# Attention scores computed once per batch, block transposes on VectorE and state rows through DRAM, in an attention and top-1 routing kernel

## Chip, cores and metric

The kernel runs on one core of a Trainium2 chip. The metric is the device time of one execution in microseconds (us); lower is better. Engines are named as in the profile: PE is TensorE (matrix products), PEld its weight loads, DVE is VectorE, ACT is ScalarE, POOL is GpSimd, SP is SyncE. PSUM is the memory that PE writes to, in eight banks of 512 float32 columns per partition; SBUF is the working memory.

## What is computed

Two blocks follow one another. The attention block has 8 batches, 8 heads, 512 tokens, 32 states and 64 dimensions per head; every token reads from the states and every state reads from the tokens:

```
scores = 0.125 * x @ state^T;   a  = softmax over the 32 states;   xread = a  @ state
scores2 = 0.125 * state @ x^T;  a2 = softmax over the 512 tokens;  sread = a2 @ x
attn_out = concatenate([xread, sread], axis=2)         # 544 rows per batch and head
```

The result, seen as 4352 rows of 512 values, goes through a switch layer with 8 experts: the row's logits are `x @ w_gate`, the expert with the largest logit is taken, and the row of the output is `gate * (relu(x @ w1[e]) @ w2[e])`, w1 being 512 by 1024 and w2 1024 by 512. Everything is float32. Note that `scores2` is `scores` transposed.

## The kernel before

The work has two stages on the same engines.

**Attention and routing** (lines 128 to 342) goes batch by batch, in a loop at lines 334 to 342. The order in which an engine gets its instructions is fixed before the run, by the framework's scheduler: it takes the instruction that is ready by its own estimate of durations, and of several the one that stands first in the program. So work of neighbouring batches is interleaved, and an engine then runs its list strictly in that order. For batch b+1 the loop calls `weights` (line 325), and then finishes batch b:

- `transpose_x` (162): 16 PE transposes (line 167) turn the tokens into columns, four to a PSUM tile, each tile copied to SBUF by `evict` (120), which takes ACT (line 124) and DVE (line 126) in turn.
- `prep_state` (149): transposes of the states (152) and state times w_gate (158).
- `read_weights` (171): 16 products with the tokens as weights and 64 state columns (line 178), in two halves of 512 score columns per partition. Then, on DVE, the maximum (181), the subtraction (183), the sum (186), a small add (187) and the reciprocal (188); on ACT the exponential (184); on POOL the scaling (189). A token lies on a partition, the states along it.
- `write_weights` (202): the same scores once more, transposed, with the states as weights (64 columns) and 512 token columns (line 209); maximum (212), exponential with the sum (215), reciprocal (217) and scaling (218).
- `transpose_read` (192) and `transpose_write` (221): 8 PE transposes each (198, 227), two PSUM tiles each, evicted into `aT` and `a2T`.
- `read_rows` (282): four tiles `px` of 512 columns (288), evicted into `row`; the logits (294) from `aT` and the product of line 158; then `route`.
- `write_rows` (302): 32 products of 32 state columns by 64 values of x (line 308), all into the 32 partitions that belong to the batch. After batches 3 and 7, 128 state rows are transposed (315), multiplied by w_gate (320) and routed.
- `route` (231): some fifteen short DVE instructions, three sets of counting products (257 to 262) and one indirect DMA on POOL's queue per 128 rows (274), which scatters the rows to their expert's place in a DRAM table. The counts in `base_e` tie each call to the one before.

A float32 product appears in the trace as two PE instructions with a weight load each, a PE transpose as one. PSUM has one set of pools for the whole kernel: `ps_m` four banks, `ps_o` two (px, pw), `ps_s` two (lines 54 to 56). SBUF tiles have two buffers, x three.

**Experts** (line 392 on): when all rows are routed, DVE works out a table of 24 tiles of 256 rows (345 to 388); then for each tile POOL gathers the rows (398), SP loads that expert's weights (407, 409), and PE does transposes (420), the up product (435) and the down product (448); rows leave by indirect DMA (452).

## Time and profile before

| | |
|---|---|
| runs | 932.76, 928.96, 931.94 us; median 931.94 |
| span of the profiled execution, first to last instruction | 925.5 us |
| PE busy | 868.1 us (94%) |
| PEld busy | 609.1 us (66%) |
| DVE busy | 219.8 us (24%) |
| POOL busy | 156.4 us (17%) |
| ACT busy | 99.4 us (11%) |

The profiled execution's own device time is not listed beside its span; the median of the three runs lies 6.4 us above the span, and that difference is taken as what lies around the span. Busy time is the time in which at least one instruction of the engine runs; instructions overlap on PE and slightly on DVE, so that a mean duration is longer than the distance between two starts. "Idle before" names what ended an engine's wait.

### The profile page before, as it was taken

The numbers are of one execution on the slowest core, as the hardware profiler recorded it, in microseconds if no ns is written. First come the engines' busy times: TensorE is split into PE (matmuls) and PEld (weight loads), VectorE is DVE, ScalarE is ACT, GpSimd is POOL, SyncE is SP. The second block draws the span as 40 slices with busy tenths as digits, with TensorE's granted clock in tenths as the row PEclk, the third lists the DMA queues.
The fourth block names the chain that finished last, engine by engine and source line by source line (L and its number), as shares of the span: only waits on it lengthen the run. The fifth ranks groups of instructions, "written<-read, shape, count | busy, mean of one in ns | idle before, by whom it ended". The sixth has DMA issues, their size and how long they took to land.

```text
span 925.5 us, 9941 instructions
## 1 busy us (share of the span) xinstructions
PE 868.1 (94%) x4028; PEld 609.1 (66%) x4028; DVE 219.8 (24%) x628; ACT 99.4 (11%) x196; POOL 156.4 (17%) x166
## 2 busy tenths in 40 slices
PE   2999999990999999999999999999999999999997
PEld 2777877780766677666677666776667766667764
DVE  4456666543111111111111111111111111111110
ACT  1223322220100000000000000000000000000000
POOL 3022332224201111011110111111111101100000
PEclk9899999995799999999999999999999999999999
DMA  9034343117754464554544535545446435355300
GB/s 159 1 84 101 93 103 92 47 47 266 268 204 165 168 215 143 198 186 148 208 171 164 215 128 204 202 136 196 153 160 216 153 146 184 112 196 178 110 0 1
DMA packets 84061, 137.06 MB, mean 148 GB/s; under 512 B 40622, under 2 KB 40622, under 8 KB 84016
## 3 DMA queue, kind: packets, MB, share of 16 engines
q1 hardware_dynamic: 70912, 109.06, 36.5%
q0 software_dynamic: 10400, 26.83, 7.7%
q10 hardware_dynamic: 2704, 0.54, 0.4%
q8 instruction: 32, 0.52, 0.2%
q14 instruction: 13, 0.11, 0.0%
HBM read 122.22 MB, written 21.53 MB: 155 GB/s over the span
## 4 chain that ended last, share of the span: by engine, by line
issue 64%; POOL 9%; PE 3%; DMA 1%; POOLq 1%; DVE 0%
POOL out_dram L452 5%; POOL xg L398 3%; PE ph L435 2%; DMA xg<-xs_dram,grow 1%; PE py L448 1%; POOL xs_dram L274 0%; POOLq L398 0%; POOLq L452 0%; POOLq L496 0%; PE ptx L420 0%; DVE y L451 0%
## 5 line engine op out<-in xcount | busy, mean ns | idle before, releaser
L435 PE MATMUL ph<-fxT,w1t 128*128 128x256 f32 x1536 | 337.4, 381 | 0.0
L448 PE MATMUL py<-w2t,hT 128*128 128x512 f32 x768 | 333.6, 592 | 0.0
L435 PEld LDWEIGHTS ph<-fxT,w1t 128*128 128x128 f32 x1536 | 293.2, 191 | 50.1 <-issue 11.0
L448 PEld LDWEIGHTS py<-w2t,hT 128*128 128x128 f32 x768 | 144.2, 190 | 172.3 <-issue 172.2
L452 POOL DMA_INDIRECT out_dram<-y,ti x48 | 48.6, 1012 | 355.5 <-DVE y L451 323.9
L451 DVE TENSOR_SCALAR y<-py,gw 128x512 f32<-128x512 f32 x48 | 36.0, 751 | 293.6 <-PE py L448 293.6
L398 POOL DMA_INDIRECT xg<-xs_dram,grow x48 | 49.5, 1030 | 252.6 <-PE ptx L420 236.8
L440 ACT ACTIVATE hT<-ph 128x512 f32<-128x512 f32 x48 | 28.7, 597 | 553.0 <-PE ph L435 553.0
L438 DVE TENSOR_SCALAR hT<-ph 128x512 f32<-128x512 f32 x48 | 33.1, 690 | 145.9 <-PE ph L435 145.9
L420 PE MATMUL ptx<-ident,xg 128*128 128x128 f32 x192 | 27.7, 288 | 22.8 <-DMA xg<-xs_dram,grow 22.8
L274 POOL DMA_INDIRECT xs_dram<-row,r_sli x32 | 31.7, 992 | 81.7 <-DVE r_sli L271 30.2
L423 DVE TENSOR_TENSOR ti<-xg,inv_i 128x1 int32<-128x1 int32 x48 | 6.0, 158 | 164.8 <-DMA out_dram<-y,ti 143.0
L420 PEld LDWEIGHTS ptx<-ident,xg 128*128 128x128 f32 x192 | 23.6, 148 | 26.6 <-issue 22.8
L178 PE MATMUL pc<-stT,xT 128*128 128x64 f32 x256 | 37.2, 307 | 0.4 <-ACT stT L124 0.4
L178 PEld LDWEIGHTS pc<-stT,xT 128*128 128x128 f32 x256 | 34.9, 219 | 2.3 <-issue 1.4
L288 PE MATMUL px<-bd,aT 128*128 128x256 f32 x128 | 31.9, 387 | 0.1
L308 PE MATMUL pw<-x_nat,a2T 128*32 128x64 f32 x512 | 30.5, 219 | 0.0
L308 PEld LDWEIGHTS pw<-x_nat,a2T 128*32 128x32 f32 x512 | 28.8, 110 | 1.5 <-ACT r_ex L247 1.3
L189 POOL TENSOR_TENSOR a<-sh,sm 128x512 f32<-128x512 f32 x16 | 16.9, 1059 | 74.9 <-DVE sm L188 73.9
L167 PE MATMUL pt<-ident,x_nat 128*128 128x128 f32 x128 | 20.7, 300 | 7.4 <-DMA x_nat<-in_x_dram 6.8
L288 PEld LDWEIGHTS px<-bd,aT 128*128 128x128 f32 x128 | 22.7, 191 | 3.3 <-DVE aT L126 0.6
L124 ACT COPY fxT<-ptx 128x512 f32<-128x512 f32 x24 | 14.0, 585 | 98.3 <-PE ptx L420 98.3
(121 smaller groups left out, 391.0 us busy)
## 6 DMA issues: line engine op xcount, KB each, us to landing
w1t<-in_moe_w_dram SPq DMA_DIRECT2D x24, 2048.0 KB, 8.9
w2t<-in_moe_w_dram SPq DMA_DIRECT2D x24, 2048.0 KB, 9.1
x_nat<-in_x_dram SPq DMA_DIRECT2D x32, 256.0 KB, 5.1
xg<-xs_dram,grow POOLq DMA_INDIRECT x48, 6.9
out_dram<-y,ti POOLq DMA_INDIRECT x48, 3.1
bd<-in_state_dram ACTq DMA_DIRECT2D x8, 64.0 KB, 4.5
xs_dram<-row,r_sli POOLq DMA_INDIRECT x32, 5.2
xs_dram<-srow,r_sli POOLq DMA_INDIRECT x2, 6.1
```

What stands on the lines that cost most here:

```text
L178: nc.tensor.matmul(pc[:, i, ts(j, 2), :], lhsT=xT[:, j, 2 * u + i, :], rhs=stT[:, b, j, :], start=True, stop=True, skip_group_check=True)
L274: d = nc.gpsimd.indirect_dma_start(out=xs_dram[:], out_offset=bass.IndirectOffsetOnAxis(ap=sli[:, u:u + 1], axis=0), in_=row[:, u, :].bitc ...
L288: nc.tensor.matmul(px[:, ts(g, 256)], lhsT=aT[:, g, c, :], rhs=bd[:, b, g], start=True, stop=True, skip_group_check=True)
L308: nc.tensor.matmul(px[r, ts(h, D)], lhsT=a2T[:, h // 4, c, ts(h % 4, NS)], rhs=x_nat[b][:, c, h, :], start=(c == 0), stop=(c == NC - 1), s ...
L398: nc.gpsimd.indirect_dma_start(out=xg_bufs[(NH * j + k) % XB][:].bitcast(I32), out_offset=None, in_=xs_dram[:], in_offset=bass.IndirectOff ...
L420: nc.tensor.transpose(pt[:, c, :], xg[:, ts(c, 128)], ident[:])
L435: nc.tensor.matmul(ph[:, i, :], lhsT=w1t[:, c, ts(2 * f2 + i, 128)], rhs=xT[:, c, :], start=(c == 0), stop=(c == NDC - 1), skip_group_chec ...
L438: nc.vector.tensor_scalar(hT[:, ts(f2, 2), :], ph[:], 0.0, None, ALU.max)
L440: nc.scalar.activation(hT[:, ts(f2, 2), :], ph[:], AF.Relu)
L448: nc.tensor.matmul(py[:], lhsT=hT[:, f, ts(k, 128)], rhs=w2t[:, f, :], start=(f == 0), stop=(f == NFC - 1))
L451: nc.vector.tensor_scalar(y[:], py[:], gw[:, k:k + 1], None, ALU.mult)
L452: d = nc.gpsimd.indirect_dma_start(out=out[:], out_offset=bass.IndirectOffsetOnAxis(ap=ti[:, k:k + 1], axis=0), in_=y[:], in_offset=None, ...
```

## The change

The scores are computed once per batch, with the states as weights (as line 209 did), into one tile of two PSUM banks. For the softmax over the states, DVE turns every 32x32 block of that tile, so that the 32 states of a head lie along the partition; it does the softmax there over 1024 columns and turns the blocks back, which gives `aT` directly. The 16 products of line 178, the 8 transposes of line 198 and the evictions of `aT` are gone. The softmax over the tokens reads the same PSUM tile; its scaling moves from the weights to the product `pw`. The write product works on pairs of heads: 16 products of 64 state columns by 128 values of x, whose two halves alternate between partitions 0 to 63 and 64 to 127; only the blocks of equal heads are kept. They are scaled from PSUM into `xs` and sent to a DRAM tile by four DMAs on ACT's queue per batch; 128 state rows are read back and routed after batch 5 (batches 0 to 3) and after the last. `write_rows` now stands before `read_rows`. PSUM pools are made anew for each stage: in the attention stage `ps_c` has two tiles of two banks, `ps_m` two banks, `ps_o` and `ps_s` one each; the expert stage has the old sizes. Comments were removed too.

```diff
+    st_dram = dram.tile([B * NS, DM], FP32)
...
-    ps_m = ctx.enter_context(tc.tile_pool(name="ps_m", bufs=4, space=bass.MemoryType.PSUM))
-    ps_o = ctx.enter_context(tc.tile_pool(name="ps_o", bufs=2, space=bass.MemoryType.PSUM))
-    ps_s = ctx.enter_context(tc.tile_pool(name="ps_s", bufs=2, space=bass.MemoryType.PSUM))
+    ps_c = tc.alloc_tile_pool(name="ps_c", bufs=2, space=PSUM)
+    ps_m = tc.alloc_tile_pool(name="ps_m", bufs=2, space=PSUM)
+    ps_o = tc.alloc_tile_pool(name="ps_o", bufs=1, space=PSUM)
+    ps_s = tc.alloc_tile_pool(name="ps_s", bufs=1, space=PSUM)
...
-    def read_weights(b, xT):
...
-    def transpose_read(a):
...
-    def write_weights(b, xT):
...
+    def scores(b, xT):
+        pc = ps_c.tile([128, 2, S], FP32, tag="c", name="pc")
+        for j in range(NPR):
+            nc.tensor.matmul(pc[ts(j % 2, 64), j // 2, :], lhsT=stT[:, b, j, :], rhs=xT[:, j],
+                             start=True, stop=True, skip_group_check=True)
+        return pc
+
+    def read_weights(pc):
+        NB = 2 * S // 32
+        sx = att.tile([128, NB, NS], FP32, tag="sx", name="sx")
+        nc.vector.transpose(sx[:].rearrange("p b n -> p (b n)"), pc[:].rearrange("p g s -> p (g s)"))
+        mx = att.tile([128, NB, 1], FP32, tag="mx", name="mx")
+        nc.vector.tensor_reduce(mx[:, :, 0], sx[:], AX.X, ALU.max)
+        nc.vector.tensor_tensor(sx[:], sx[:], mx[:].to_broadcast([128, NB, NS]), ALU.subtract)
+        nc.scalar.activation(sx[:], sx[:], AF.Exp, bias=0.0, scale=SCALE)
+        sm = att.tile([128, NB, 1], FP32, tag="sm", name="sm")
+        nc.vector.tensor_reduce(sm[:, :, 0], sx[:], AX.X, ALU.add)
+        nc.vector.tensor_scalar(sm[:], sm[:], 1e-9, None, ALU.add)
+        nc.vector.reciprocal(sm[:], sm[:])
+        nc.gpsimd.tensor_tensor(sx[:], sx[:], sm[:].to_broadcast([128, NB, NS]), ALU.mult)
+        aT = att.tile([128, 2, NC, 128], FP32, tag="aT", name="aT")
+        nc.vector.transpose(aT[:].rearrange("p g c q -> p (g c q)"), sx[:].rearrange("p b n -> p (b n)"))
+        return aT
+
+    def write_weights(pc):
+        nm = att.tile([128, 2], FP32, tag="nm", name="nm")
+        nc.vector.tensor_reduce(nm[:], pc[:], AX.X, ALU.max)
+        nc.vector.tensor_scalar(nm[:], nm[:], -SCALE, None, ALU.mult)
+        a2 = att.tile([128, 2, S], FP32, tag="a2", name="a2")
+        s2 = att.tile([128, 2], FP32, tag="s2", name="s2")
         for g in range(2):
+            nc.scalar.activation(a2[:, g], pc[:, g], AF.Exp, bias=nm[:, g:g + 1], scale=SCALE,
+                                 accum_out=s2[:, g:g + 1])
+        nc.vector.tensor_scalar(s2[:], s2[:], 1e-9, None, ALU.add)
+        nc.vector.reciprocal(s2[:], s2[:])
+        return a2, s2
...
-    def write_rows(b, a2T):
...
+    def write_rows(b, a2T, s2):
+        pw = ps_o.tile([128, 2, 2, D], FP32, tag="o", name="pw")
+        for g in range(2):
             for c in range(NC):
+                for i in range(2):
+                    nc.tensor.matmul(pw[ts(i, 64), g], lhsT=a2T[:, g, c, ts(i, 64)],
+                                     rhs=x_nat[b][:, c, ts(2 * g + i, 2), :],
+                                     start=(c == 0), stop=(c == NC - 1), skip_group_check=True)
+        xs = att.tile([128, 2, 2, D], FP32, tag="xs", name="xs")
+        for g in range(2):
+            nc.vector.tensor_scalar(xs[:, g], pw[:, g], s2[:, g:g + 1], None, ALU.mult)
+        for i in range(4):
+            nc.scalar.dma_start(out=st_dram[ts(b, NS)].rearrange("n (g i d) -> n g i d", g=2, i=4)[:, :, i, :],
+                                in_=xs[ts(i, NS), :, i % 2, :])
+
+    def route_states(g4):
+        srow = att.tile([128, 1, XW], FP32, tag="srow", bufs=1, name="srow")
+        nc.scalar.dma_start(out=srow[:, 0, 0:DM], in_=st_dram[ts(g4, 128)])
...
     def weights(b):
         xT = transpose_x(b)
         prep_state(b)
-        return read_weights(b, xT), write_weights(b, xT)
+        pc = scores(b, xT)
+        return read_weights(pc), write_weights(pc)
...
-        a, a2 = soft
+        aT, (a2, s2) = soft
...
-        aT = transpose_read(a)
         a2T = transpose_write(a2)
+        write_rows(b, a2T, s2)
         read_rows(b, aT)
-        write_rows(b, a2T)
+        if b == 5:
+            route_states(0)
+    route_states(1)
...
-    att.release()
+    for pool in (ps_s, ps_o, ps_m, ps_c, att):
+        pool.release()
...
+    ps_m = tc.alloc_tile_pool(name="ps_m2", bufs=4, space=PSUM)
+    ps_o = tc.alloc_tile_pool(name="ps_o2", bufs=2, space=PSUM)
+    ps_s = tc.alloc_tile_pool(name="ps_s2", bufs=2, space=PSUM)
```

What `route_states` does after its DMA is what lines 314 to 323 did.

## Rows read from the trace of the kernel before

**Rows 1.** The page's span in 40 slices, busy tenths of each: PE, DVE.

```profile
PE   2999999990999999999999999999999999999997
DVE  4456666543111111111111111111111111111110
```

**Rows 2.** By stretch: us, busy PE, PEld, DVE, ACT, POOL, granted clock, DMA share, GB/s.

```profile
56.70:77.92 21.22, 20.16 (x190) 17.18 (x189) 13.28 (x43) 6.87 (x15) 6.20 (x6) 1.00 0.46 101
...
168.08:191.20 23.12, 21.40 (x190) 17.41 (x189) 13.86 (x42) 6.68 (x16) 6.06 (x6) 1.00 0.12 46
...
206.05:238.30 32.25, 7.17 (x42) 5.35 (x42) 10.65 (x62) 2.19 (x5) 14.78 (x15) 0.58 0.77 278
238.30:925.50 687.20, 682.19 (x2479) 456.79 (x2477) 92.34 (x205) 41.53 (x70) 88.19 (x87) 1.00 0.46 162
```

**Rows 3.** PE in order of time, one batch (start, us, what, idle before).

```profile
168.08 3.76 PE L308 MATMUL pw<-x_nat,a2T 128*32 128x64 f32 x64
171.77 1.86 PE L167 MATMUL pt<-ident,x_nat 128*128 128x128 f32 x15
...
175.16 0.66 PE L178 MATMUL pc<-stT,xT 128*128 128x64 f32 x4
...
176.75 3.34 PE L178 MATMUL pc<-stT,xT 128*128 128x64 f32 x28
...
181.88 0.66 PE L198 MATMUL pt<-ident,a 128*128 128x128 f32 x4
183.16 0.63 PE L198 MATMUL pt<-ident,a 128*128 128x128 f32 x4 [0.62 <-DVE nm L213]
...
185.86 1.99 PE L288 MATMUL px<-bd,aT 128*128 128x256 f32 x8
187.69 1.40 PE L294 MATMUL pl<-gst,aT 128*128 128x8 f32 x12
```

**Rows 4.** PE in order of time: eight instructions of line 209; a hand-over of a bank.

```profile
109.60 1.94 PE L209 MATMUL pc<-xT,stT 128*64 128x512 f32 x8
...
112.80 0.66 PE L198 MATMUL pt<-ident,a 128*128 128x128 f32 x4 [0.68 <-ACT aT L124]
```

**Rows 5.** Groups by line and shape, 98.98 to 181.5 us (busy us, mean ns).

```profile
L126 DVE COPY row<-px 128x512 f32<-128x512 f32 x7 | 4.8, 691 | 6.0 <-PE px L288 6.0
...
L218 DVE TENSOR_SCALAR a<-a,s 128x512 f32<-128x512 f32 x6 | 2.6, 433 | 0.0
L187 DVE TENSOR_SCALAR sm<-sm 128x16 f32<-128x16 f32 x6 | 2.4, 406 | 0.0
...
L126 DVE COPY stT<-pt 128x128 f32<-128x128 f32 x4 | 1.1, 286 | 0.2
...
L184 ACT ACTIVATE sh<-sh 128x512 f32<-128x512 f32 x7 | 4.4, 630 | 18.1 <-DVE sh L183 18.1
```

**Rows 6.** POOL and DVE around 114 us, in order of time.

```profile
113.67 1.04 POOL L189 TENSOR_TENSOR a<-sh,sm 128x512 f32<-128x512 f32 x1 [2.94 <-DVE sm L188]
...
114.10 0.64 DVE L187 TENSOR_SCALAR sm<-sm 128x16 f32<-128x16 f32 x1
```

**Rows 7.** Line 136, DMA issues on ACT's queue: duration ns min/median/max; landing.

```profile
L136 ACTq DMA_DIRECT2D bd<-in_state_dram x8: 318/330/472, 10.4 to 16.7; - x8
...
DMA to landing us min/median/max: 4.2/4.5/5.5
```

**Rows 8.** The first batch in order of time.

```profile
22.59 1.12 PE L178 MATMUL pc<-stT,xT 128*128 128x64 f32 x4
...
30.33 3.68 PE L209 MATMUL pc<-xT,stT 128*64 128x512 f32 x8
...
50.37 1.03 PE L288 MATMUL px<-bd,aT 128*128 128x256 f32 x4
```

**Rows 9.** Two stretches of 2 us in the first batch (granted clock third from last).

```profile
36.00:38.00 2.00, 1.41 (x11) 0.87 (x9) 2.00 (x7) 1.30 (x4) 1.01 (x2) 1.00 0.03 8
...
42.00:44.00 2.00, 2.00 (x11) 2.00 (x11) 1.35 (x2) 0.50 (x1) 0.00 (x0) 0.50 0.00 0
```

More of the change, by code (lines that the diff above doesn't have):

```diff
@@ L53 @@
     wpool = ctx.enter_context(tc.tile_pool(name="wpool", bufs=2))
[L54 to L56 removed]
+    PSUM = bass.MemoryType.PSUM
     xs_dram = dram.tile([E * NTOK, XW], I32)
+    st_dram = dram.tile([B * NS, DM], FP32)
     ident = const.tile([128, 128], FP32)
@@ L192, in transpose_read @@
-    def transpose_read(a):
-        aT = att.tile([128, 2, NC, 128], FP32, tag="aT", name="aT")
-        for g in range(2):
-            pt = ps_m.tile([128, NC, 128], FP32, tag="m", name="pt")
-            for c in range(NC):
-                nc.tensor.transpose(pt[:, c, :], a[:, c, ts(g, 4), :], ident[:])
-            evict(aT[:, g], pt[:])
-        return aT
-    def write_weights(b, xT):
-        a2 = att.tile([128, 2, S], FP32, tag="a2", name="a2")
-        for g in range(2):
-            pc = ps_m.tile([128, S], FP32, tag="m", name="pc2")
-            for i in range(2):
-                j = 2 * g + i
-                nc.tensor.matmul(pc[ts(i, 64), :], lhsT=stT[:, b, j, :], rhs=xT[:, j],
-                                 start=True, stop=True, skip_group_check=True)
-            nm = att.tile([128, 1], FP32, tag="nm", name="nm")
-            nc.vector.tensor_reduce(nm[:], pc[:], AX.X, ALU.max)
-            nc.vector.tensor_scalar(nm[:], nm[:], -SCALE, None, ALU.mult)
-            s2 = att.tile([128, 1], FP32, tag="s2", name="s2")
-            nc.scalar.activation(a2[:, g], pc[:], AF.Exp, bias=nm[:, 0:1], scale=SCALE, accum_out=s2[:])
-            nc.vector.tensor_scalar(s2[:], s2[:], 1e-9, None, ALU.add)
-            nc.vector.reciprocal(s2[:], s2[:])
-            nc.vector.tensor_scalar(a2[:, g], a2[:, g], s2[:, 0:1], None, ALU.mult)
-        return a2
@@ L296, in read_rows @@
         route(pl[:], row, tok_x[:, b, :], NC)
-    srow = {}
-    def write_rows(b, a2T):
-        g4, r = b // 4, ds(NS * (b % 4), NS)
-        if b % 4 == 0:
-            srow[g4] = att.tile([128, 1, XW], FP32, tag="srow", name="srow")
-        px = ps_o.tile([128, DM], FP32, tag="o", name="pw")
-        for h in range(H):
-            for c in range(NC):
-                nc.tensor.matmul(px[r, ts(h, D)], lhsT=a2T[:, h // 4, c, ts(h % 4, NS)],
-                                 rhs=x_nat[b][:, c, h, :], start=(c == 0), stop=(c == NC - 1),
-                                 skip_group_check=True)
-        evict(srow[g4][r, 0, 0:DM], px[r, :])
-        if b % 4 == 3:
-            pt = ps_m.tile([128, NDC, 128], FP32, tag="m", name="pt")
-            for c in range(NDC):
-                nc.tensor.transpose(pt[:, c, :], srow[g4][:, 0, ts(c, 128)], ident[:])
-            sT = att.tile([128, NDC, 128], FP32, tag="sT", bufs=1, name="sT")
-            evict(sT[:], pt[:])
-            pl = ps_s.tile([128, 1, E], FP32, tag="s", name="pls")
-            for c in range(NDC):
-                nc.tensor.matmul(pl[:, 0, :], lhsT=sT[:, c, :], rhs=wg[:, c, :],
-                                 start=(c == 0), stop=(c == NDC - 1), skip_group_check=True)
-            route(pl[:], srow[g4], tok_s[:, g4:g4 + 1], 1)
@@ new lines, in route_states @@
+    def route_states(g4):
+        srow = att.tile([128, 1, XW], FP32, tag="srow", bufs=1, name="srow")
+        nc.scalar.dma_start(out=srow[:, 0, 0:DM], in_=st_dram[ts(g4, 128)])
+        pt = ps_m.tile([128, NDC, 128], FP32, tag="m", name="pt")
+        for c in range(NDC):
+            nc.tensor.transpose(pt[:, c, :], srow[:, 0, ts(c, 128)], ident[:])
+        sT = att.tile([128, NDC, 128], FP32, tag="sT", bufs=1, name="sT")
+        evict(sT[:], pt[:])
+        pl = ps_s.tile([128, 1, E], FP32, tag="s", name="pls")
+        for c in range(NDC):
+            nc.tensor.matmul(pl[:, 0, :], lhsT=sT[:, c, :], rhs=wg[:, c, :],
+                             start=(c == 0), stop=(c == NDC - 1), skip_group_check=True)
+        route(pl[:], srow, tok_s[:, g4:g4 + 1], 1)
@@ L468 @@
             fetch(j + 2)
-    ffn.release()
+    for pool in (ps_s, ps_o, ps_m, ffn):
+        pool.release()
 _INS = ['x', 'state', 'moe_w_gate', 'moe_w1', 'moe_w2']
```

18 lines of the change are left out of this document (removed).

## Prediction

> **What bounds the kernel now.** I read the 40 slices first [rows 1]: PE is at nine tenths from the second slice to the last but for one hole near 215 to 230 us, and DVE is at five or six tenths in the first eight slices only. So there are two stages. I then cut the span into stretches [rows 2]. The experts take 687.2 us with PE busy in 682.2 of them; the diff gives this stage the PSUM banks that it had, so I leave it alone. The attention stage is six intervals from the write product of batch 0 (56.70) to that of batch 6 (191.20), 134.5 us or 22.4 us each, with PE busy in some 93% and DVE in about 60%. [Rows 2] show the first and the last of the six. A PE-bound stage is the right place to remove PE work. Between 206.05 and 238.30 PE waits for the last scatters, the tile table and the first gathered rows; that tail goes on.
>
> **The change, part by part, per interval, on PE's queue.**
>
> *Read scores removed.* Line 178 is 32 PE instructions per batch, 0.66 + 3.34 us [rows 3], with about 0.1 of overlap: **−3.9**. Line 209, which stays, gives all the scores in 1.94 us [rows 4].
>
> *Transposes of the read weights removed.* They fill 181.88 to 183.79 [rows 3], 1.3 of work and 0.6 of wait: **−1.9**. The wait on the write weights that follows stays.
>
> *Write product by pairs.* Now 64 instructions in 3.76 us [rows 3], that is 4096 columns. After it 32 instructions of 128 columns, again 4096, but alternating between two halves of the partitions. The nearest row is line 209, eight of 512 columns alternating the same way: 4096 columns in 1.94 [rows 4]. The ends are 1.94 and 3.76 (nothing runs side by side). The instructions are four times shorter than line 209's and each brings a weight load, so I take 2.5: **−1.3**.
>
> *One bank for px and pw.* Each of the five tiles per batch must now be evicted before the next may start. The one hand-over of this kind in the trace cost PE 0.68 us behind an ACT copy [rows 4]; behind a DVE copy of 0.69 [rows 5] about 0.8. Five at 0.75 are 3.75. The cover is work that the scheduler can put there: logits (12 of 16 instructions in 1.40, so 1.85 for all) and the transposes of the next x (1.86 [rows 3]). Ends 0 and 3.75, and above this if an eviction queues behind a long DVE instruction; I take **+1.3**.
>
> *Two banks in place of four* for the seven tiles of transposes: four transposes take 0.45 to 0.65, a hand-over 0.75, so with two banks each tile exposes about 0.2, if back to back 1.4; I take **+0.8**, ends 0 and 2.8 (0.4 each).
>
> *DVE.* Two copies [rows 5] give the slope: (691 − 286) ns over 384 columns is 1.05 ns a column, so an instruction of 1024 columns takes 0.69 + 0.54 = 1.23. Per interval DVE is busy 13.3 to 13.9 now [rows 2]. Added: two block turns, for which the trace has no row; at a copy's rate 2 x 1.23 = 2.46 (below a copy would need a cheaper pass than any here; above, four passes each would be about 2 x 4.4). Four passes of 1024 in place of eight of 512: 4.92 − 5.52 = −0.6. Gone: line 218, 2 x 0.43 [rows 5]; one aT eviction, 0.69; a share of the pw eviction, 0.26; about half of the small instructions, 0.5 (line 187 alone 2 x 0.41 [rows 5]). Added: two scalings of 128 columns, 0.57. Net about +0.1, so some 13.5 of an 18 us interval. The Trainium skill (VectorE: DVE Perf Modes, The three transpose paths) lists 311 ns for a 128x128 bf16 block turn; eight of those, an estimate, would be 2.5 us per turn and DVE's sum 16. No run here shows it yet.
>
> *DVE beside POOL.* An add of 16 columns took 0.64 us at 114.10 while POOL's scaling ran from 113.67 to 114.71 [rows 6]; it ended as POOL did. POOL's instruction is now one of 1024 columns, so 2.1 us by twice its row. What can meet it are the small adds, for up to 2.1 each interval; I take 0.5. The Trainium skill (SBUF — State Buffer, Who interferes with whom) says that a DVE instruction with two SBUF inputs is blocked too by a POOL instruction that reads SBUF. By that rule the new subtraction, which reads sx and mx from SBUF where line 183 read PSUM, joins those that can wait. By it DVE could lose up to another 2.1 in an interval, and DVE's sum would be 15.6, still below 18; the trace of before has no such pair.
>
> *ACT.* Four DMA issues of 0.33 [rows 7] are 1.3 us on ACT's queue per batch, against two fewer copies of 0.6; ACT is busy 6.9 of 21 [rows 2], so no cost by itself. But these issues wait for xs, and evictions behind them wait too, and long DVE passes hold evictions: **+0.6** for PE, for both.
>
> Sum per interval: −3.9 − 1.9 − 1.3 + 1.3 + 0.8 + 0.6 = −4.4, an interval of 18.0. Six: **−26.4**.
>
> **Start.** Products of the first batch run at about half the later rate: line 209 takes 3.68 [rows 8] where it takes 1.94 later [rows 4]. Batch 0's px starts at 50.37. After: from 22.6, scores 3.7, turn 1.23, maximum 1.23, subtraction 1.23, exponential 1.2 (under twice line 184's 0.63 [rows 5]), sum 1.2, small ones 0.5, scaling 2.1, turn 1.23 make 13.6; with 0.5 of hand-overs and 2.5 for batch 1's evictions and the write maximum in between, px starts near 39. The write product fits into the wait. That is −11.4, and pw (3.76) no longer follows px, but px pays three hand-overs (2.3): **−13**; ends −8 and −16.
>
> **Last batch.** 14.85 now, from 191.20 to 206.05 [rows 2]: two write products −2.6, transposes −1.3, hand-overs with only the logits as cover +1.9: **−2**.
>
> **Tail.** State rows go to DRAM and back. The nearest landing is 4.2 to 5.5 us [rows 7], twice that with the issues about 10. It lies beside four px (7 us), logits and route, since the write product now comes first; what is late next is routing, no longer covered by pw: **+1**, ends 0 and +5. The first state group is routed two batches later than before, its data long landed: 0.
>
> **Sum:** −26.4 − 13 − 2 + 1 = −40.4, a span of 885.1. The median lies 6.4 above the span of before, so 891.5; I say **892**.
>
> **Rivals.**
>
> *The clock falls.* In the first batch, after a stretch of transposes and waits with PE busy 1.41 of 2 us, the granted clock went to 0.50, the 1.2 GHz level, and stayed there while PE was busy throughout [rows 9]. Gaps return if the hand-overs are not covered. Against it: at 93% the clock reads 1.00 in every interval [rows 2]. If a third of the 108 us of six intervals ran at half, 18 us of work would be lost and some 6 of it met by idle time: +12, **904**.
>
> *DVE becomes the bound.* It decides once a block turn takes over 3.5 us (13.5 − 2.5 + 7 = 18). At four passes, 4.4 to 5 us, plus POOL's full 2.1 per interval, DVE would need 21 to 22: +3.5 x 6, +8 in the start's chain and +6 at the end, **927**. For: DVE's share rises to three quarters. Against: all DVE passes in the trace go at one rate.
>
> *The single bank eats more than was removed.* Place: px and pw in ps_o. If a hand-over has no cover, and those on DVE queue behind a 1.23 us pass (0.8 + 1.2 = 2.0 for half of them, 0.7 for the rest), five cost 6.8; ps_m at its end 2.8, ACT's and DVE's queues 0.6. That gives +3.1 in place of −4.4: 6 x 3.1 = +19, start −9, last batch +3, tail +2, so about **947**. It decides for slower when these three together pass 7.1 by more than about 2 per interval. For: ps_o goes from two banks to one. Against: 3.7 us of independent PE work per batch, and a scheduler that already puts x transposes among px.
>
> *The pairs don't run side by side*: pw stays 3.76, +1.3 eight times: 902, inside my range.
>
> **How the numbers follow.** Forecast 0.71 (with the pairs' case), clock 0.12, DVE 0.06, single bank 0.11. The range: with every stall covered and pw at 1.94 the sum is −7.6 x 6 − 16 − 3, so 867; I take 872 as the low end. The high end takes in the clock's case with half of the stage slow (about 910) and part of the DVE case: 920. Runs of before differ by 0.4%, so 0.5% is about what a measurement tells from no change: faster is below 927.3, slower above 936.6. Forecast and clock give faster, 0.83; the DVE case same, 0.06; the bank slower, 0.11.
>
> **What would show it.** Right: starts of the write product about 18 us apart; pw near 2.5 us; block turns near 1.23; DVE busy 13 to 14 per interval; PE's idle before px ended by row evictions and below 2 us per batch; granted clock 1.00 from about 50 us on; an unchanged 687 us of experts. Wrong: turns above 3 us; px separated by 1.5 us or more with nothing between; a clock of 0.5 inside the intervals; the table (line 345 of before) waiting for the DMA of srow.

## Result and the profile after

The changed kernel takes **899.38 us** (median of 4 runs, 899.31 to 899.81), the kernel before 930.61 us beside it (4 runs, 928.96 to 932.76): ratio 0.967, 95% interval 0.962 to 0.971. That is faster, 7 us above the 892 forecast and inside the range. I cut both profiled executions at the first px of batch 0, the first px of batch 6 and the first up product of the experts:

| stretch, us | before | after | difference | predicted |
|---|---|---|---|---|
| start to px of batch 0 | 50.37 | 53.07 | +2.7 | −13 (−11.4 of it before this px) |
| six intervals, px of batch 0 to px of batch 6 | 135.49 | 108.05 | −27.4 | −26.4 |
| px of batch 6 to the first up product | 52.46 | 49.00 | −3.5 | −1 |
| experts | 687.18 | 687.88 | +0.7 | 0 |
| span | 925.5 | 898.0 | −27.5 | −40.4 |

The profiled execution of after took 899.81 us, 1.8 more than its span. In the 20 later runs of before, too, time and span are 1.7 to 1.8 us apart. So the 6.4 us that I set around the span of before was mostly something else: that execution, some 927.3 us long, was itself about 4.6 us quicker than its median, and quicker than every run of before that was timed.

The page of after, 40 slices of 22 us (PE, DVE, granted clock), to be read against [rows 1]:

```profile
PE   3788898729999999999999999999999999999997
DVE  4584878531111111111111111111111111111100
PEclk9888999666999999999999999999999999999999
```

PE has fallen from nine tenths to eight in the attention stage, DVE has risen to eight in some slices, and the clock is below full in several. By stretch, with the columns of [rows 2], after:

```profile
53.07:161.12 108.05, 91.20 (x693) 67.48 (x691) 81.16 (x209) 32.71 (x73) 35.48 (x31) 0.95 0.44 115
161.12:185.80 24.68, 19.12 (x104) 14.09 (x104) 9.40 (x39) 3.63 (x10) 8.68 (x8) 0.72 0.25 73
185.80:210.12 24.32, 8.02 (x37) 5.49 (x36) 9.62 (x55) 1.97 (x4) 12.51 (x14) 0.56 0.69 258
210.12:898.00 687.88, 682.92 (x2475) 457.30 (x2475) 92.16 (x202) 41.53 (x70) 87.50 (x86) 0.99 0.47 165
```

and the same six intervals of before:

```profile
50.37:185.86 135.49, 126.78 (x1149) 105.33 (x1147) 83.86 (x273) 42.60 (x97) 37.96 (x38) 1.00 0.36 89
```

An interval is 18.0 us (108.05 / 6), as forecast; DVE is busy 13.5 of them (81.16 / 6), as forecast. PE's busy time fell by 35.6 us in the six intervals, its idle time rose from 8.7 to 16.9. What PE did in them, and what ended its waits (busy us, mean ns, idle before), after:

```profile
L282 PE MATMUL px<-bd,aT 128*128 128x256 f32 x97 | 28.8, 421 | 7.4 <-DVE xs L304 2.8 <-ACT row L123 2.4 <-DVE row L125 1.7
L179 PE MATMUL pc<-xT,stT 128*64 128x512 f32 x48 | 16.2, 607 | 0.0
...
L299 PE MATMUL pw<-x_nat,a2T 128*64 128x128 f32 x192 | 13.9, 295 | 2.6 <-DVE a2T L125 2.6
```

before:

```profile
L288 PE MATMUL px<-bd,aT 128*128 128x256 f32 x96 | 23.9, 385 | 0.1
L308 PE MATMUL pw<-x_nat,a2T 128*32 128x64 f32 x384 | 22.9, 220 | 0.0
```

px, which PE used to run without a wait, now waits 7.4 us, 6.9 of it for evictions out of the one bank. Its busy time grew by 4.9 us. Only two of its 24 tiles there ran at half clock, 1.92 and 1.91 us long, which makes some 1.8 of the 4.9; most of the rest is that a tile now stands alone and takes 1.03 to 1.13 us, where two in a row took 1.99 [rows 3]:

```profile
72.80 1.92 PE L282 MATMUL px<-bd,aT 128*128 128x256 f32 x4
```

**Start.** PE in order of time, after:

```profile
39.75 1.09 PE L299 MATMUL pw<-x_nat,a2T 128*64 128x128 f32 x16
...
45.37 3.58 PE L288 MATMUL pl<-gst,aT 128*128 128x8 f32 x16 [2.56 <-DVE aT L198]
48.88 1.98 PE L299 MATMUL pw<-x_nat,a2T 128*64 128x128 f32 x16
...
53.07 1.03 PE L282 MATMUL px<-bd,aT 128*128 128x256 f32 x4
```

and DVE beside it:

```profile
36.46 0.17 DVE L125 COPY gst<-pg 128x16 f32<-128x16 f32 x1 [2.43 <-PE pg L162]
36.55 1.21 DVE L193 TENSOR_REDUCE sm<-sx 128x32 f32<-128x1024 f32 x1
39.27 1.25 DVE L187 STREAM_TRANSPOSE sx<-pc 128x1024 f32<-128x1024 f32 x1 [1.50 <-PE pc L179]
...
41.63 0.34 DVE L195 RECIPROCAL sm<-sm 128x32 f32<-128x32 f32 x1
...
44.07 1.25 DVE L198 STREAM_TRANSPOSE aT<-sx 128x1024 f32<-128x1024 f32 x1 [1.02 <-POOL sx L196]
...
46.41 0.68 DVE L125 COPY a2T<-pt 128x512 f32<-128x512 f32 x1
...
51.33 0.33 DVE L304 TENSOR_SCALAR xs<-pw,s 128x128 f32<-128x128 f32 x1
```

DVE first waited 2.43 us for the copy of batch 1's `gst`, whose product stood behind batch 1's first scores on PE. The sum of batch 0 was done at 37.8, its reciprocal came 3.9 us later: batch 1's turn and first maximum stand ahead of it on DVE's list. `aT` was ready at 45.32 and px started 7.75 us after that. The only bank had been opened by the first half of pw at 39.75; the second half needed the `a2T` tile copied at 46.41 and ran at 48.88, behind the logits at half clock; xs freed the bank at 51.66, and more transposes stood on PE between that and px. PE was not idle in these 7.75 us (busy 7.59): its list put the logits, pw's second half and transposes ahead of px.

**The end.** POOL's scatters and the first gather of the experts, after:

```profile
181.19 0.98 POOL L268 DMA_INDIRECT xs_dram<-row,r_sli  x1 [5.40 <-DVE row L125]
...
186.72 0.97 POOL L268 DMA_INDIRECT xs_dram<-row,r_sli  x1 [0.83 <-ACT row L123]
191.50 0.97 POOL L268 DMA_INDIRECT xs_dram<-srow,r_sli  x1 [3.81 <-DVE nt_i L351]
195.61 1.05 POOL L405 DMA_INDIRECT xg<-xs_dram,grow  x1 [3.13 <-DVE loc L386]
```

The logits come from `aT` and are done before px, so the slots are known and the last four scatters go out as each px is evicted; only the state scatter comes after them. From the first px of batch 7 to the first up product it is 31.0 us where it was 41.7 (from the last px 24.7 where it was 38.0). But batch 7's px now comes 18.0 us after batch 6's (179.08 − 161.12), where it was 10.7 before (196.59 − 185.86). The two together are the −3.5. PE, before and then after:

```profile
196.59 0.60 PE L288 MATMUL px<-bd,aT 128*128 128x256 f32 x2
```

```profile
179.08 1.10 PE L282 MATMUL px<-bd,aT 128*128 128x256 f32 x4 [0.81 <-DVE xs L304]
```

### The profile page after: what moved, and what is told of

The parts are those of the page before. It is cut to its first block, busy times and chain, and to the rows that moved or that the text cites. A ratio compares the mean times of both kernels' runs of the same rounds, so it can differ in the third digit from the quotient of the medians.

```text
span 898.0 us, 8743 instructions
## 1 busy us (share of the span) xinstructions
PE 832.9 (93%) x3452; PEld 565.0 (63%) x3452; DVE 220.4 (25%) x560; ACT 90.6 (10%) x176; POOL 154.9 (17%) x158
## 3 DMA queue, kind: packets, MB, share of 16 engines
q1 hardware_dynamic: 70912, 109.06, 37.8%
## 4 chain that ended last, share of the span: by engine, by line
issue 65%; POOL 8%; DMA 2%; PE 2%; POOLq 1%; DVE 0%; DVEq 0%
POOL out_dram L459 5%; POOL xg L405 3%; PE ph L442 2%; DMA xg<-xs_dram,grow 1%; DMA w1t<-in_moe_w_dram 1%; POOLq L405 0%; POOLq L459 0%; POOLq L504 0%; DMA xs_dram<-srow,r_sli 0%; DVE ti L430 0%; DVE gw L432 0%; DVEq L430 0%
## 5 line engine op out<-in xcount | busy, mean ns | idle before, releaser
L442 PEld LDWEIGHTS ph<-fxT,w1t 128*128 128x128 f32 x1536 | 293.8, 191 | 50.6 <-issue 11.4
L282 PE MATMUL px<-bd,aT 128*128 128x256 f32 x128 | 39.9, 439 | 11.6 <-DVE row L125 4.5
L430 DVE TENSOR_TENSOR ti<-xg,inv_i 128x1 int32<-128x1 int32 x48 | 6.0, 157 | 168.2 <-DMA out_dram<-y,ti 154.3
L171 PE MATMUL pt<-ident,x_nat 128*128 128x128 f32 x128 | 26.4, 342 | 11.5 <-DMA x_nat<-in_x_dram 6.6
L171 PEld LDWEIGHTS pt<-ident,x_nat 128*128 128x128 f32 x128 | 18.7, 174 | 18.5 <-issue 7.2
L196 POOL TENSOR_TENSOR sx<-sx,sm 128x1024 f32<-128x1024 f32 x8 | 15.3, 1912 | 68.9 <-ACT xT L123 33.7
L179 PE MATMUL pc<-xT,stT 128*64 128x512 f32 x64 | 24.9, 705 | 0.0
L299 PE MATMUL pw<-x_nat,a2T 128*64 128x128 f32 x256 | 20.6, 318 | 3.1 <-DVE a2T L125 2.6
L299 PEld LDWEIGHTS pw<-x_nat,a2T 128*64 128x64 f32 x256 | 17.8, 161 | 4.7 <-DVE a2T L125 2.9
```

The lines of the kernel that those rows point to most:

```text
L171: nc.tensor.transpose(pt[:, c, :], x_nat[b][:, c, ts(j, 2), :], ident[:])
L282: nc.tensor.matmul(px[:, ts(g, 256)], lhsT=aT[:, g, c, :], rhs=bd[:, b, g], start=True, stop=True, skip_group_check=True)
L299: nc.tensor.matmul(pw[ts(i, 64), g], lhsT=a2T[:, g, c, ts(i, 64)], rhs=x_nat[b][:, c, ts(2 * g + i, 2), :], start=(c == 0), stop=(c == NC ...
L442: nc.tensor.matmul(ph[:, i, :], lhsT=w1t[:, c, ts(2 * f2 + i, 128)], rhs=xT[:, c, :], start=(c == 0), stop=(c == NDC - 1), skip_group_chec ...
```

## Experiments

The kernel before took 938.7, 940.2 and 941.8 us (medians) beside the three sets of four kernels, while the changed kernel came back at 899.54. So verdicts are given as ratios, and variants of the changed kernel are also set against each other in us. The table gives the profile of each: px of batch 0; first to last px, with PE's busy us and clock there; last px to the first up product. The profile of before is the quick execution named above: it lies 11 to 15 us below the medians of before beside the variants, so that gains read against it are too small, and losses too large, by about that, and no profile shows where those 11 to 15 us would stand. The tail counts from the last px, so it also shrinks where that px merely comes later.

| kernel | us | ratio (95%) | start | first to last px (PE busy, clock) | tail |
|---|---|---|---|---|---|
| before | 930.61 | 1 | 50.4 | 149.9 (141.2, 1.00) | 38.0 |
| after | 899.38 | 0.967 (0.962 to 0.971) | 53.1 | 132.3 (109.9, 0.91) | 24.7 |
| after again | 899.54 | 0.957 (0.951 to 0.964) | 52.4 | 134.5 (110.2, 0.91) | 24.1 |
| write part alone | 918.08 | 0.978 (0.970 to 0.986) | 52.6 | 149.4 (138.1, 0.95) | 28.5 |
| read part alone | 917.57 | 0.979 (0.973 to 0.986) | 43.1 | 156.1 (134.8, 0.87) | 29.7 |
| before, PSUM cut | 956.43 | 1.017 (1.013 to 1.021) | 56.6 | 181.4 (153.1, 0.94) | 28.5 |
| two px banks | 887.73 | 0.947 (0.941 to 0.953) | 38.5 | 131.8 (112.6, 0.92) | 29.2 |
| two px banks, SP queue | 895.90 | 0.953 (0.947 to 0.960) | 38.0 | 138.5 (113.6, 0.89) | 30.3 |
| SP queue | 899.18 | 0.956 (0.953 to 0.959) | 50.3 | 133.7 (118.0, 0.87) | 24.1 |
| extra turn | 906.08 | 0.966 (0.960 to 0.973) | 57.2 | 134.9 (111.8, 0.89) | 25.0 |
| read first | 925.68 | 0.983 (0.979 to 0.987) | 44.5 | 154.3 (128.4, 0.79) | 37.1 |
| read first, two px banks | 908.63 | 0.967 (0.961 to 0.973) | 43.7 | 135.8 (116.4, 0.90) | 39.4 |
| the same with idle products | 903.05 | 0.961 (0.955 to 0.967) | 43.7 | 132.0 (123.4, 0.95) | 38.2 |
| four groups | 907.81 | 0.965 (0.962 to 0.969) | 51.2 | 140.1 (114.3, 0.84) | 24.1 |

The intervals of the write part, the read part, the PSUM cut and read first leave out 1 but reach over 2%: these four differ from before, and whether by 2% is open.

### The two halves of the change

The write part alone, on the kernel before with its PSUM pools:

```diff
+        pw = ps_o.tile([128, 2, 2, D], FP32, tag="o", name="pw")
...
+                for i in range(2):
+                    nc.tensor.matmul(pw[ts(i, 64), g], lhsT=a2T[:, g, c, ts(i, 64)],
+                                     rhs=x_nat[b][:, c, ts(2 * g + i, 2), :],
...
+        evict(xs[:], pw[:])
+        for i in range(4):
+            nc.scalar.dma_start(out=st_dram[ts(b, NS)].rearrange("n (g i d) -> n g i d", g=2, i=4)[:, :, i, :],
+                                in_=xs[ts(i, NS), :, i % 2, :])
...
+        write_rows(b, a2T)
         read_rows(b, aT)
-        write_rows(b, a2T)
+        if b == 5:
+            route_states(0)
+    route_states(1)
```

> The kernel before with the write part of the change alone: pairs of heads, rows through DRAM, write rows ahead of read rows; old softmax over the states, old PSUM pools. Theory A (what is removed from PE's queue is what is gained): pw goes from 3.76 to 1.97 us, so 1.8 us per batch or 14 us, and the tail gets 8 to 10 us shorter because the last rows are scattered as their px tiles are evicted: 905 to 912. Rival: the tail's gain comes from the logits that the block turns give early, not from the order; then this kernel gains the 14 us of pw alone, about 917.

The read part alone, the changed kernel with the old `write_rows` (line 302 of before), the old order and a2 scaled on DVE:

```diff
+            nc.vector.tensor_scalar(a2[:, g], a2[:, g], s2[:, g:g + 1], None, ALU.mult)
...
-    def write_rows(b, a2T, s2):
+    def write_rows(b, a2T):
...
-        write_rows(b, a2T, s2)
         read_rows(b, aT)
+        write_rows(b, a2T)
```

> The changed kernel with the old write part: heads one by one into 32 partitions, weights scaled, rows kept in SBUF, read rows first. Theory A: the scores and transposes removed are worth 5.8 us per batch less 2 to 3 of waits for one px bank, some 20 us, and the tail is the old one: 908 to 915. Rival B (VectorE is the bound in the middle of the stage, where its busy share is 77 to 95 per cent): the longer pw is hidden beside VectorE's work, so only the tail is lost, 900 to 908.

Beside a before of 938.7 they gain 20.6 and 21.1 us; both together gain 42.2 beside 941.8. So the halves add up, as far as the spread of the runs of before (931 to 945 us in these sets) can tell. As gains, both fit their theory A (18.6 to 25.6 and 15.6 to 22.6); the times in us that go with these theories counted from 930.6. Where each half gains is not settled: beside the profile of before, the write part's is 9.5 us shorter in the tail and hardly shorter between the px, the read part's 7 us shorter in the start and 8 in the tail and longer between the px, but the spans differ by 7.5 and 10.0 us only, and the PSUM cut below, which gains nothing, has a tail of 28.5 too. What the read part's own profile shows is that its stretch between the px, 156.1 us, holds new waits, though 16 products (32 PE instructions) and 8 transposes per batch are gone: px waits 16.5 us there, 11.9 of it for rows to leave the one bank and 4.0 for `aT`, and the clock reads 0.87.

```profile
L283 PE MATMUL px<-bd,aT 128*128 128x256 f32 x128 | 43.1, 462 | 16.5 <-DVE row L124 8.2 <-DVE aT L197 4.0 <-ACT row L122 3.7
```

### The PSUM banks

The kernel before with the change's small pools (its scores lie in `ps_m` too, so this cut is harder than the change's):

```diff
-    ps_m = ctx.enter_context(tc.tile_pool(name="ps_m", bufs=4, space=bass.MemoryType.PSUM))
-    ps_o = ctx.enter_context(tc.tile_pool(name="ps_o", bufs=2, space=bass.MemoryType.PSUM))
-    ps_s = ctx.enter_context(tc.tile_pool(name="ps_s", bufs=2, space=bass.MemoryType.PSUM))
...
+    ps_m = tc.alloc_tile_pool(name="ps_m", bufs=2, space=PSUM)
+    ps_o = tc.alloc_tile_pool(name="ps_o", bufs=1, space=PSUM)
+    ps_s = tc.alloc_tile_pool(name="ps_s", bufs=1, space=PSUM)
```

> The kernel before with the attention stage's PSUM cut to the changed kernel's split: two banks for transposes, one for px and pw, one small, four left empty. This prices the smaller pools where DVE is not loaded. Theory A: 2 to 4 us per batch, 945 to 960 against 930.6. Rival: the scheduler covers the hand-overs, 930 to 936.

It is slower than before by 1.7%, 16.2 us beside a before of 940.2: the low end of theory A's 2 to 4 us per batch. Beside the profile of before the stretch between the px is 31.5 us longer and the span 27.7, of which some 12 is that execution's quickness. Then the changed kernel with its eight banks shared out otherwise:

```diff
-    ps_c = tc.alloc_tile_pool(name="ps_c", bufs=2, space=PSUM)
-    ps_m = tc.alloc_tile_pool(name="ps_m", bufs=2, space=PSUM)
-    ps_o = tc.alloc_tile_pool(name="ps_o", bufs=1, space=PSUM)
+    ps_c = tc.alloc_tile_pool(name="ps_c", bufs=1, space=PSUM)
+    ps_m = tc.alloc_tile_pool(name="ps_m", bufs=3, space=PSUM)
+    ps_o = tc.alloc_tile_pool(name="ps_o", bufs=2, space=PSUM)
```

> The changed kernel with the eight PSUM banks dealt out otherwise: two for px and pw, three for transposes, one score tile of two banks in place of two tiles. Rival C (one bank for px and pw costs PE its waits for row evictions): those waits, 12 us in all in the changed kernel, go, so 886 to 893. If instead VectorE sets the pace (rival B), no more than 3 us go: 896 to 900. With a single score tile the next batch's scores must wait for the exponential of this one; if that is the tighter limit, slower than 900.

**887.73 us**, the fastest kernel of this study, 11.7 below the changed one. PE at its first px:

```profile
37.20 1.09 PE L299 MATMUL pw<-x_nat,a2T 128*64 128x128 f32 x16
38.49 1.13 PE L282 MATMUL px<-bd,aT 128*128 128x256 f32 x4 [0.19 <-DVE aT L198]
```

px starts 0.19 us behind the turn that gives `aT`, at 38.5 where the forecast had 39, with the second half of pw still open in the other bank. The time is rival C's, but the gain did not come from the waits that it named. The start gains 14.6 us, the tail gives back 4.5, the stretch between hardly moves: px's waits fall from 11.6 to 3.9 us there, but others grow. The spare banks are worth their time in the first batch.

### Order of the two products

```diff
-        write_rows(b, a2T, s2)
         read_rows(b, aT)
+        write_rows(b, a2T, s2)
```

> The changed kernel with read rows ahead of write rows again, nothing else. If the shorter tail comes from the order (the last four scatters start as px is evicted, before the state rows), it is lost: 8 to 10 us, 907 to 910. If it comes from the logits being computed before px whatever the order, the tail stays, and the state rows' way through DRAM now lies bare at the end: 3 to 8 us more, 902 to 907.

26.3 us slower than the changed kernel, beyond both expectations: 22 of them between the px, 12.4 in the tail, 8.6 won in the start. Is it the bank or the order? The same with two px banks (`ps_c` 1, `ps_o` 2; one bank lies unused):

```diff
-    ps_c = tc.alloc_tile_pool(name="ps_c", bufs=2, space=PSUM)
+    ps_c = tc.alloc_tile_pool(name="ps_c", bufs=1, space=PSUM)
...
-    ps_o = tc.alloc_tile_pool(name="ps_o", bufs=1, space=PSUM)
+    ps_o = tc.alloc_tile_pool(name="ps_o", bufs=2, space=PSUM)
...
-        write_rows(b, a2T, s2)
         read_rows(b, aT)
+        write_rows(b, a2T, s2)
```

> The changed kernel with the read product ahead of the write rows, and the banks split so that px has two, the transposes two, the scores one, and one bank lies unused. Base of the next run. As the read-first kernel of before, the granted clock from the first px to the last should be 0.75 to 0.85, that stretch 145 to 156 us, the ratio 0.975 to 0.99. If that kernel's loss came from its single px bank instead, px is now evicted beside the next one, and the stretch falls to 130 to 136 us.

The stretch between the px comes back to 135.8, the clock to 0.90: that loss was the bank's, and the second theory holds. The tail stays at 39.4: that is the order's together with the state rows' way through DRAM, which now stands last, so that PE waits 12.40 us for it:

```profile
194.14 1.12 PE L315 MATMUL pt<-ident,srow 128*128 128x128 f32 x4 [12.40 <-DMA srow<-st_dram]
```

The read part alone, which also puts the read product first but keeps the state rows in SBUF, has a tail of 29.7. With the write product first, the one px bank does little harm between the px (132.3 us, and 131.8 with two), and the tail is 10 to 12 us shorter with the same number of px banks.

These two kernels also part the two sizes in the first batch. pw is not in px's way here, and px starts as `aT` is ready, at 44.45 with one px bank and at 43.72 with two, still with two banks for transposes; with three it was 38.49. PE in the two, one px bank first:

```profile
44.45 2.08 PE L282 MATMUL px<-bd,aT 128*128 128x256 f32 x4 [3.73 <-DVE aT L198]
```

```profile
43.72 4.54 PE L282 MATMUL px<-bd,aT 128*128 128x256 f32 x12 [3.73 <-DVE aT L198]
```

### Does PE's clock cost time?

The kernel just shown, with a product that nobody reads into the unused bank before each px:

```diff
+            nc.tensor.matmul(pf[:], lhsT=ident[:], rhs=a2T[:, c % 2, 0:3, :], start=True, stop=True,
+                             skip_group_check=True)
```

> The kernel of the run before this one with one product of 384 columns, whose result nobody reads, into the unused bank before each px: 4 per batch, 32 in all, by the rows for 512 columns (1.0 us at full clock) about 0.75 us each, 24 us of PE work at full clock. If PE's low granted clock is a cause of time and follows from PE's gaps, the clock in the middle rises to 0.9 or more, the px fall from about 2.0 to 1.1 us, and the time stays within 5 us of the run before or falls. If the low clock is only a companion of waits that set the time, the filler fits into the gaps at no cost and the clock changes little. If PE's work sets the time whatever its clock, the time rises by 20 us or more.

Between the first and the last px, without the idle products (the stretch with the columns of [rows 2], then PE's groups):

```profile
43.72:179.84 136.12, 116.73 (x824) 84.78 (x826) 96.05 (x256) 39.08 (x87) 41.64 (x36) 0.90 0.39 98
```

```profile
L282 PE MATMUL px<-bd,aT 128*128 128x256 f32 x128 | 37.7, 432 | 9.7 <-DVE aT L198 9.0 <-ACT row L123 0.7
L179 PE MATMUL pc<-xT,stT 128*64 128x512 f32 x48 | 23.3, 779 | 1.1 <-ACT stT L123 1.1
```

and with them:

```profile
43.73:176.10 132.37, 123.79 (x863) 91.37 (x863) 93.47 (x245) 39.72 (x86) 42.06 (x36) 0.95 0.40 104
```

```profile
L286 PE MATMUL px<-bd,aT 128*128 128x256 f32 x127 | 35.8, 413 | 6.8 <-DVE aT L200 6.2 <-DVE row L247 0.3 <-DVE r_sli L267 0.3
L283 PE MATMUL pf<-a2T,ident 128*128 128x384 f32 x62 | 24.9, 533 | 1.1 <-DVE a2T L125 1.1
L181 PE MATMUL pc<-xT,stT 128*64 128x512 f32 x48 | 15.8, 606 | 0.8 <-ACT stT L123 0.8
```

24.9 us of useless work on PE, and the kernel is 5.6 us faster (902.3 to 904.0 for 907.1 to 909.9), not 20 us slower. So PE's work does not set the time between the px here, and the clock rose as the gaps were filled: the same number of score products takes 15.8 us in place of 23.3, with less of them at half clock, 1.2 GHz. That the half clock costs the kernel 5.6 us is not shown. px hardly changed (a mean of 413 ns for 432), and DVE's list came out in another order: batch 1's `aT` is turned at 53.0 us in place of 54.7, ahead of other work. Nor does the clock follow PE's idle share alone over the kernels of the table: between the px the PSUM cut is idle for 16% at a clock of 0.94, the SP queue's kernel for 12% at 0.87. The reverse case takes work away, with pw by single heads in four groups of 32 partitions (64 instructions of 64 columns in place of 32 of 128; their blocks are then all kept):

```diff
-                for i in range(2):
-                    nc.tensor.matmul(pw[ts(i, 64), g], lhsT=a2T[:, g, c, ts(i, 64)],
-                                     rhs=x_nat[b][:, c, ts(2 * g + i, 2), :],
+                for i in range(4):
+                    nc.tensor.matmul(pw[ts(i, NS), g], lhsT=a2T[:, g, c, ts(i, NS)],
+                                     rhs=x_nat[b][:, c, 4 * g + i, :],
```

> The changed kernel with the write product by single heads, each in its own 32 partitions, so that four column groups alternate and nothing is computed in vain: 64 instructions of 64 columns per batch in place of 32 of 128. If products in different partitions run side by side, two or four deep, pw takes 1 to 2 us in place of 1.97 and the time is within 2 us or 5 us lower. If the weight loads bind (64 loads of 0.056 us, the rate of the old pw), pw takes 3.6 us again and about 1.6 us per batch are lost where PE is the bound: 905 to 912.

Between its first and last px, and its product there:

```profile
51.20:191.30 140.10, 114.33 (x1019) 80.62 (x1018) 95.42 (x247) 36.27 (x81) 44.38 (x39) 0.84 0.36 100
```

```profile
L299 PE MATMUL pw<-x_nat,a2T 128*32 128x64 f32 x448 | 12.1, 257 | 2.5 <-issue 1.1 <-ACT row L123 0.7 <-DVE a2T L125 0.4
```

The product's busy time between the px falls from 17.6 to 12.1 us, and the kernel is 8.4 us slower, at a clock of 0.84: the time of the second expectation without its cause. Together with the idle products this speaks for PE's work no longer being what sets the time in this stage.

### Is it DVE, or ACT's queue?

```diff
         nc.vector.transpose(aT[:].rearrange("p g c q -> p (g c q)"), sx[:].rearrange("p b n -> p (b n)"))
+        nc.vector.transpose(aT[:].rearrange("p g c q -> p (g c q)"), sx[:].rearrange("p b n -> p (b n)"))
```

> The changed kernel with every turn back into aT done twice: 1.24 us more on VectorE per batch, nothing else. Theory A (VectorE has room): it costs 0 to 3 us in all. Rival B (VectorE is the bound): 8 x 1.24 = 10 us, so 909.

DVE's groups from 50 to 190 us, of this kernel:

```profile
L198 DVE STREAM_TRANSPOSE aT<-sx 128x1024 f32<-128x1024 f32 x7 | 8.7, 1236 | 1.9 <-POOL sx L196 1.9
L199 DVE STREAM_TRANSPOSE aT<-sx 128x1024 f32<-128x1024 f32 x7 | 8.6, 1226 | 0.0
...
L187 DVE STREAM_TRANSPOSE sx<-pc 128x1024 f32<-128x1024 f32 x6 | 7.4, 1241 | 4.5 <-PE pc L179 4.5
```

8.6 us more on DVE lengthen the stretch between the px by 2.6 (by 0.4 against the repeated run); the waits before the turns, 5.2 and 7.7 us in the changed kernel, take up most of it. The start grows by 4.1, more than its two extra turns (2.5). In all it is 6.7 us, between the 3 and the 10 of the two expectations: between the px DVE is near the bound but not it, and this run alone does not settle it for the whole.

The state transfers issued by SP in place of ACT:

```diff
-            nc.scalar.dma_start(out=st_dram[ts(b, NS)].rearrange("n (g i d) -> n g i d", g=2, i=4)[:, :, i, :],
+            nc.sync.dma_start(out=st_dram[ts(b, NS)].rearrange("n (g i d) -> n g i d", g=2, i=4)[:, :, i, :],
...
-        nc.scalar.dma_start(out=srow[:, 0, 0:DM], in_=st_dram[ts(g4, 128)])
+        nc.sync.dma_start(out=srow[:, 0, 0:DM], in_=st_dram[ts(g4, 128)])
```

> The changed kernel with the state rows' DMAs issued on SyncE's queue in place of ScalarE's, nothing else. If the issues and their waits hold up evictions on ScalarE (2.5 us of issues per batch in the trace, and one wait of 3.1 us for the read back at the end), 3 to 8 us go: 891 to 896. If ScalarE has room, within 1.5 us of 899.4; the loads of x queued behind the waits on SyncE could cost a little.

899.18 us, the changed kernel's time, as the second expectation had it: ACT's four issues per batch and two reads back cost nothing that these runs tell. The same edit on the kernel with two px banks (both diffs are above):

> The changed kernel with the second px bank and third transposes bank of the earlier experiment, and in addition the state transfers and the rows' fetch issued by SyncE. If the gains of the two edits add (start: px of batch 0 at about 38 to 39 us; the ACT queue relieved of five issues per batch), the ratio is 0.935 to 0.942, the span 883 to 886. If the ACT queue's issues were covered by PE's own work in the middle, the ratio stays at 0.945 to 0.95 as with the banks alone, span 886 to 889.

895.90, slower than 887.73 and outside both expectations. The start is as good (38.0), but 6.7 us are lost between the px. They are lost at batch 6, whose px starts at 162.6 for 148.5 and which regains part of it; up to batch 5 the two kernels are within 1.4 us. There, of this kernel, DVE and then PE:

```profile
154.30 0.68 DVE L125 COPY a2T<-pt 128x512 f32<-128x512 f32 x1
```

```profile
144.02 0.66 PE L221 MATMUL pt<-ident,a 128*128 128x128 f32 x4
...
155.03 1.97 PE L299 MATMUL pw<-x_nat,a2T 128*64 128x128 f32 x14 [0.51 <-DVE a2T L125]
```

The last tile of `a2T` lay ready in PSUM from 144.7, and DVE copied it at 154.30, behind two routings and the next batch's softmax. In the kernel with ACT's queue the same copy follows its product at once:

```profile
144.01 0.68 DVE L125 COPY a2T<-pt 128x512 f32<-128x512 f32 x1
```

SP's queue does not touch that copy, and no wait of PE before the products of x is ended by a load of x, which SP also issues; the scheduler's fixed order came out otherwise. So an edit can move this stage by some 7 us through the order alone, and the smaller differences above (the extra turn's 6.7, four groups' 8.4, the idle products' 5.6) carry that doubt: in each of these kernels DVE's list has another order.

The unedited changed kernel in the same set:

> The changed kernel once more, unedited, beside the three above on the same chip. The ratio is 0.963 to 0.971 if a chip only scales both kernels, and its difference to the run with two px banks and SyncE is that edit's worth with no chip between them. If the ratio moves by more than 0.5%, the ratios of runs on different chips can't be set against each other to better than that.

899.54 us: against 899.38 it repeats to 0.02%, with DVE's, POOL's and PE's lists in the same order, but its ratio is 0.957 in place of 0.967, since the kernel before was slower there. Ratios of different sets can't be set against each other to better than 1%; as far as this one repeat tells, times of the changed kernel's variants can.

## Why the prediction was right, and where it failed

- **The interval, right.** −4.4 forecast, (108.05 − 135.49) / 6 = −4.57 measured (up to 0.8 more if the 4.6 us by which that execution of before was quick lie here). PE's busy time fell by 5.9 per interval. The pairs run side by side entirely, 1.97 us at full clock, not the 2.5 taken; the low end, 1.94, was the right row.
- **PE's idle time, nearly right.** The bank, the two `ps_m` banks and the queueing were to add 2.7 and a wait of 0.6 to go; idle rose by 1.4 per interval. The half clock, not in the sum, took back up to 0.9 per interval: 0.95 is a tenth of 108 us at half speed, so up to 5.4 us of work.
- **DVE's budget, right.** 13.5 forecast and measured, a turn 1.24 us for 1.23. The Trainium skill (VectorE: DVE Perf Modes, The three transpose paths) has 311 ns for a 128x128 bf16 turn; the estimate of 2.5 us made from it is twice what the rows show, so the copy's rate was the better row.
- **The start, wrong.** This is the step that failed: −13 forecast, +2.7 measured. Of the −13, 1.6 fall behind px of batch 0; px itself was forecast for 39.2 and came at 53.07. These 13.9 us are more than the whole 12.9 by which the span came out too long. Of them, 2.3 is that the scores start at 24.9 and not 22.6 (they came at 23.95 with three `ps_m` banks; before had four), 3.8 the longer chain (batch 1's passes ahead of batch 0's on DVE's list), 7.75 the bank. I priced a bank at its hand-over, 0.75. But pw, placed first, holds it from its first product to its eviction, through its own wait for the second `a2T` tile: 39.75 to 51.66. With two px and three transposes banks px starts at 38.5, 14.5 us after the scores where 16.6 were costed, so the chain of passes itself was costed well enough. The read-first kernels part the two sizes: without pw in its way px starts at 44.45 and 43.72 with two transposes banks, so pw's hold of the bank is the 7.75, and some 5 go with the third transposes bank (the order of the two products is the other difference). The forecast priced the transposes' banks per tile in the intervals and gave the start nothing for them beyond 0.5 of hand-overs; with two of them a copy of batch 1's `stT` stands at 32.06 among batch 0's passes on DVE, with three all copies of `stT` are done by 24.0, before these passes.
- **The end, right in sum by two errors.** −1 forecast, −3.5 measured. That routing runs before px, and scatters go out with it, goes with 11 us less from batch 7's px on and was not in the sum; nor was it that batch 7's px comes 7 us later after batch 6's. That they nearly cancel is luck. The srow transfer cost what was said, little: PE waited 0.59 us for it.
- **The time around the span, wrong by 4.6.** With 1.8 the forecast would have been 886.9. The 6.4 hid 4.6 of the span's 12.9.
- **The rivals.** *The clock falls* came in part: half speed for a tenth of the six intervals, not a third, but for over half of the last 25 us (0.72). The sign "granted clock 1.00 from about 50 us on" failed with it. *DVE becomes the bound* did not: turns took 1.24 us, and an extra one per batch was mostly taken up by waits between the px. *The single bank* did not eat the gain in the intervals, but it did in the start, and with the read product first it does between the px (154.3 us for 149.9 before). *Pairs not side by side* did not.

The last batch shows the two costs at once, a px waiting for the bank and a product at half clock (PE, after):

```profile
165.66 2.08 PE L282 MATMUL px<-bd,aT 128*128 128x256 f32 x4 [0.40 <-DVE row L125]
...
174.59 3.68 PE L299 MATMUL pw<-x_nat,a2T 128*64 128x128 f32 x32 [0.48 <-ACT row L123]
...
180.97 1.13 PE L282 MATMUL px<-bd,aT 128*128 128x256 f32 x4 [0.78 <-DVE row L125]
```

pw is 3.68 us here and 1.97 at full clock, a px tile 2.08 and 1.13.

## What to carry to other kernels

Price a PSUM bank by how long its product holds it, from the first partial product to the eviction and through every wait between, and look for the place where it tells: here the first batch, not the steady interval. When PE work is removed from a stage that it bounds, ask what PE does in the gaps: here part of its products then ran at half clock; and once PE is no longer the bound, less PE work need not be less time, and more of it need not be more. And make the sum against the profiled execution's own time; where that isn't listed, don't take the distance to the median for something that lies around the span.

## What was not expected of the hardware

- **Useless products that cost nothing.** 24.9 us more PE work in 132 us, a clock of 0.95 for 0.90, and 5.6 us less time, which the order of DVE's list may explain as well as the clock.
- **Small DVE instructions that end with POOL's.** POOL and DVE in order of time, after:

```profile
93.03 1.91 POOL L196 TENSOR_TENSOR sx<-sx,sm 128x1024 f32<-128x1024 f32 x1 [10.15 <-DVE r_cand L233]
```

```profile
53.12 0.91 DVE L233 SCALAR_TENSOR_TENSOR r_cand<-r_sh,rev 128x32 f32<-128x32 f32 x1
...
93.76 1.19 DVE L246 COPY row<-tok_x 128x4 int32<-128x4 int32 x1
...
143.03 1.44 DVE L211 TENSOR_SCALAR s<-s 128x2 f32<-128x2 f32 x1
```

A copy of four values takes 1.19 us, where it takes 0.16 otherwise, and ends as POOL's scaling does; the other two end with scalings that began at 52.06 and 142.52. With 162.89 (0.54 us) that is four in eight batches, 3.4 us too long in all, 0.4 per batch where 0.5 was taken. Not every one is held: a sum at 93.59, inside the same scaling, took 0.19. The Trainium skill (SBUF — State Buffer, Who interferes with whom) says that a DVE instruction with two SBUF inputs contends with a POOL instruction that reads SBUF; line 233 agrees. Lines 211 and 246 have one input; the same section counts `copy` and `tensor_scalar`, which these are, among those that can contend when their operands meet certain conditions, and no run here tests those. The subtraction of line 190, the case that I had weighed, never met POOL (1183 to 1217 ns in all eight).
- **The kernel before varies from set to set more than the changed one.** In the three later sets the runs of before took 931 to 945 us, at mean granted clocks of 0.955 to 0.977 (931.32 us at 0.977, 944.68 at 0.959); its medians go from 930.6 to 941.8. The changed kernel, run in the first and the last set, has medians of 899.38 and 899.54 and single runs from 897.7 to 902.7. No run here shows why.
